# A retention layer with a phase MLP behind it: which transposes run on TensorE, which tiles go ahead, where stores are issued

## The chip, the cores and the metric

The kernel runs on one core of one Trainium2 chip. The metric is the device time of one execution in microseconds. Of the kernel before, 13 executions are known; their median is 204.08 us.

The engines of the core are called PE (matrix products, and transposes as products with an identity matrix), DVE (VectorE), ACT (ScalarE), POOL (GpSimd) and SP (SyncE, which here only issues DMAs). Each works through its own list of instructions in order. The DMA engines move data between memory and the chip, and within the chip; a DMA can also transpose a block of 16-bit numbers on the way.

## The reference, cut to what matters

```python
# q, k, v: 4 batches, 8 heads, 768 positions, 64 numbers each
for t in range(S):
    state = gamma * state + outer(k[t], v[t])        # per batch and head, 64 x 64
    y[t] = scale * q[t] @ state
x = y with the heads side by side                    # 4 x 768 x 512
theta = x @ w_theta
zr, zi = x * cos(theta), x * sin(theta)
u = x + (w_tok_r @ zr + w_tok_i @ zi)                # sums over the 768 positions of a batch
out = u + maximum(u @ w_ch, 0)
```

The second half of the work mixes all positions of a batch, so nothing of a batch's output can be computed until its retention part is complete.

## The kernel before, in words

**Tiling.** The 768 positions of a batch are six tiles of 128. Two tiles make a pair, so there are three pairs in a batch and twelve in all (n = 0 to 11, nG = 3). Output tiles are numbered m = 0 to 23, six in a batch.

**Retention, per pair.** `load` brings k, q and v of a pair (512 KB each). `prep` casts k to bf16 on ACT, and scales and casts q and v on POOL (in the first pairs half of q on DVE). q and k are then needed transposed: `flip` does it with eight TensorE transposes into PSUM and a DVE copy (kqT, L184), `flip_dma` with one DMA that transposes (L189). `ret_A` computes scores (L202), `ret_mask` masks them on DVE (L209), `ret_Y` multiplies with v (L225), `ret_I` adds the contribution of the state (L239), `ret_S` updates the state (L256) and copies it on ACT (L264). `ret_out` copies the transposed result xT out of PSUM (L273). x itself, with positions on the partitions, comes out of xT by `x_pe` (four TensorE transposes and a DVE copy, L286 and L287) or by `x_dma` (a DMA, L278).

**The MLP, per tile.** `theta` is four products (L293) and two ACT calls for cosine and sine; `zmul` multiplies them with x on DVE (L303). `moe_M` sums twelve products over the batch (L315), `moe_u` adds x on DVE (L322). u is transposed for the last product by `moe_U_dma`, a DMA (L327). `moe_O` is four products with w_ch (L333), `moe_out` the maximum and the sum on DVE, and the store, issued on SP (L340, L341).

**Weights.** `w_cast` (POOL) and `w_tok` (TensorE transposes, and copies on DVE and ACT) prepare a row block of the two token matrices.

**The order** is written out by hand and taken as it stands by each engine. First a ramp for pairs 0 to 2, line by line, with unneeded products in it (`keep_busy`). Then a loop over n = 3 to 12: slot n does the first half of pair n's retention, the second half of pair n-1's, theta and zmul of pair n-1, the MLP sums of the tiles in `tiles_of[n]`, and `moe_O` and `moe_out` of the tiles of slot n-1. Before, `tiles_of` has tiles 0 and 1 in slot 3, 2 and 3 in slot 4, 4 in slot 5, 5 in slot 6, and two in each slot after. A last loop does the six tiles of the last batch, and `moe_last` the final one.

**PSUM.** Pools are named by tag. Tag "tr" has two buffers, which `flip`, `x_pe`, `w_tok`, `moe_O` and, from pair 3 on, `theta` take in turn: a use can begin once the copy of the use two before is done. Tag "y" (the sums of `moe_M`) has one buffer.

**SP's order in a slot**, before: load k of pair n+2, the DMA transposes of u of slot n-1's tiles, that of x of pair n-1, load q, the DMA transpose of k of pair n+1, load v, that of q of pair n+1, and the stores at the end. What stands behind an instruction that waits on SP waits too.

Of the kernel before, what the change touches and what calls it, by code (L numbers as in the profile page):

```python
# [15 lines left out]
BF = mybir.dt.bfloat16  # L16
# [16 lines left out]
def kernel(  # L33
# [17 lines left out]
    nc = tc.nc  # L51
# [8 lines left out]
    gammas = [1.0 - 2.0 ** (-5.0 - h) for h in range(H)]  # L60
    nG = nT // 2

    ctx.enter_context(tc.manual_schedule())

    const = ctx.enter_context(tc.tile_pool(name="const", bufs=1))
# [30 lines left out]
    def loads(order):  # L96
        for what in order.split():
            if what == "th":
                load_w512("th", moe_w_theta)
            elif what == "ch":  # L100
                load_w512("ch", moe_w_ch)
            elif what[0] == "w":
                for r in range(2):
                    load_wtok(r, int(what[1:]))
            else:
                for name in "kqv":
                    load(int(what[1:]), name)

    loads("p0 th p1 w0 p2 w1 w2 p3 w3 p4 ch")


    warm = const.tile([P, dm], BF)
# [169 lines left out]
    def x_pe(n, a):  # L282
        b, g = divmod(n, nG)
        x_ps = psum.tile([P, NP, P], BF, name="x_ps", tag="tr", bufs=2)
        for j in range(NP):
            nc.tensor.transpose(x_ps[:, j, :], st[n, "xT"][:, a, j, :], ident)  # L286
        nc.vector.tensor_copy(xs[b][:, 2 * g + a, :], x_ps.rearrange("p j e -> p (j e)"))  # L287
# [12 lines left out]
    def zmul(n, a):  # L300
        b, g = divmod(n, nG)
        c = 2 * g + a
        nc.vector.tensor_mul(zs[b][:, c], st[n, "cs", a], _bcast_mid(xs[b][:, c, :], 2))  # L303
# [21 lines left out]
    def moe_U_dma(m):  # L325
        uT = work.tile([P, nD, P], BF, name="uT", bufs=4)
        nc.sync.dma_start_transpose(out=uT, in_=mo[m]["u"])  # L327
        mo[m]["uT"] = uT

    def moe_O(m):  # L330
        o_ps = psum.tile([P, dm], FT, name="o_ps", tag="tr", bufs=2)
        for j in range(nD):
            nc.tensor.matmul(o_ps, mo[m]["uT"][:, j, :], wch[:, j, :], start=(j == 0),  # L333
                             stop=(j == nD - 1))
        mo[m]["o"] = o_ps

    def moe_out(m):
        b, t0 = divmod(m, nT)
        ot = work.tile([P, dm], FT, name="ot", bufs=4)
        nc.vector.scalar_tensor_tensor(ot, mo[m]["o"], 0.0, mo[m]["u"], ALU.max, ALU.add)  # L340
        nc.sync.dma_start(out=out[b, t0 * P:(t0 + 1) * P, :], in_=ot)  # L341

    wrow = {}

# [18 lines left out]
    def moe_last(m):  # L363

        b, t0 = divmod(m, nT)
        hw = dm // 2
        y_ps = [psum.tile([P, hw], FT, name="y_ps", tag="y", bufs=1),
                psum.tile([P, hw], FT, name="y_ps", tag="acc", bufs=2)]
        u = work.tile([P, dm], BF, name="u", bufs=5)
        uT = work.tile([P, nD, P], BF, name="uT", bufs=4)  # L370

        def prods(e):
            for s0 in range(nT):
                for r in range(2):
                    nc.tensor.matmul(y_ps[e], wT[r][:, s0, t0 * P:(t0 + 1) * P],  # L375
                                     zs[b][:, s0, r, e * hw:(e + 1) * hw],
                                     start=(s0 == 0 and r == 0),
                                     stop=(s0 == nT - 1 and r == 1))
            nc.vector.tensor_add(u[:, e * hw:(e + 1) * hw], y_ps[e],
                                 xs[b][:, t0, e * hw:(e + 1) * hw])  # L380

        def flip_u(e):
            u_ps = psum.tile([P, 2, P], BF, name="u_ps", tag="tr", bufs=2)
            for j in range(2):
                jj = 2 * e + j
                nc.tensor.transpose(u_ps[:, j, :], u[:, jj * P:(jj + 1) * P], ident)
            nc.scalar.copy(uT[:, 2 * e:2 * e + 2, :], u_ps)

        moe_U_dma(m - 1)
        prods(0)  # L390
        moe_O(m - 2)
        moe_out(m - 2)
        prods(1)
        flip_u(0)
        moe_O(m - 1)
        moe_out(m - 1)
        flip_u(1)
        o_ps = [psum.tile([P, hw], FT, name="o_ps", tag="st", bufs=1),
                psum.tile([P, hw], FT, name="o_ps", tag="acc", bufs=2)]
        for js in ((0, 1), (2, 3)):  # L400
            for e in range(2):
                for j in js:
                    nc.tensor.matmul(o_ps[e], uT[:, j, :],
                                     wch[:, j, e * hw:(e + 1) * hw], start=(j == 0),
                                     stop=(j == nD - 1))
        for e in range(2):
            ot = work.tile([P, hw], FT, name="oh", bufs=2)
            nc.vector.scalar_tensor_tensor(ot, o_ps[e], 0.0, u[:, e * hw:(e + 1) * hw],
                                           ALU.max, ALU.add)
            (nc.sync, nc.scalar)[e].dma_start(  # L410
                out=out[b, t0 * P:(t0 + 1) * P, e * hw:(e + 1) * hw], in_=ot)
# [44 lines left out]
    w_cast(0)  # L456
    ret_A(1, 0)
    ret_mask(1, 0)
    prep(2, "k", K)
    keep_busy(2)  # L460
    ret_S(1, 0)
    zmul(0, 0)
    ret_A(1, 1)
    ret_mask(1, 1)
    ret_Y(1, 0)
    ret_I(1, 0)
    ret_S(1, 1)
    flip(2, "k")
    ret_I(1, 1)
    ret_Y(1, 1)  # L470
    ret_out(1, 0, nc.scalar.copy)
    ret_out(1, 1, nc.scalar.copy)
    prep(2, "q", DP)
    w_tok(0)
    zmul(0, 1)
    x_pe(1, 0)
    theta(1, 0)
    flip(2, "q")
    prep(2, "v", PP)
    w_cast(1)  # L480
    w_cast(2)
    x_pe(1, 1)
    theta(1, 1)
    ret_A(2, 0)
    ret_mask(2, 0)
    moe_M(0, 0, 2)
    ret_A(2, 1)
    ret_mask(2, 1)
    ret_S(2, 0)
    ret_Y(2, 0)  # L490
    ret_I(2, 0)
    ret_I(2, 1)
    prep(3, "k", K)
    ret_Y(2, 1)
    ret_out(2, 0, nc.scalar.copy)
    ret_out(2, 1, nc.scalar.copy)
    zmul(1, 0)
    w_tok(1)
    zmul(1, 1)
    prep(3, "q", DP)  # L500
    prep(3, "v", PP)
    x_pe(2, 0)
    theta(2, 0)
    moe_M(0, 2, 4)
    x_pe(2, 1)
    theta(2, 1)
    flip(3, "k")
    flip(3, "q")
    w_tok(2)
    zmul(2, 0)  # L510
    zmul(2, 1)


    tiles_of = {nG: [0, 1], nG + 1: [2, 3], nG + 2: [4], nG + 3: [5]}
    m = nT
    for n in range(nG + 4, B * nG + 1):
        tiles_of[n] = [m, m + 1]
        m += 2
    pairs = range(B * nG)
    for n in range(nG, B * nG + 1):  # L520
        mine = tiles_of[n]
        done = tiles_of.get(n - 1, [])
        late = n > nG
        if n + 2 in pairs:
            load(n + 2, "k")
        for t in done:
            moe_U_dma(t)
        if n + 1 in pairs:
            prep(n + 1, "q", PP)
            prep(n + 1, "v", PP)  # L530
        if n == nG:
            w_cast(3)
        if n in (nG + 1, nG + 2):
            w_cast(n - nG + 3)
        if n == nG + 1:
            nc.gpsimd.tensor_copy(wch, wdma["ch"])
        if late:
            ret_I(n - 1, 1)

        if n in pairs:  # L540
            ret_A(n, 0)
            ret_mask(n, 0)
        if late:
            ret_Y(n - 1, 1)
            ret_S(n - 1, 1)
            ret_out(n - 1, 0, nc.scalar.copy)
            ret_out(n - 1, 1, nc.scalar.copy)
            x_dma(n - 1)
        if n + 2 in pairs:
            load(n + 2, "q")  # L550
        if n + 1 in pairs:
            prep(n + 1, "k", K)
            flip_dma(n + 1, "k")
        if n == nG:
            moe_M(0, 4, nT)
        else:
            moe_M(mine[0], 0, nT // 2)
            theta(n - 1, 0)
            moe_M(mine[0], nT // 2, nT)
        if n == nG + 1:  # L560
            w_tok(3)
        moe_u(mine[0])
        if n + 2 in pairs:
            load(n + 2, "v")
        if n + 1 in pairs:
            flip_dma(n + 1, "q")
        if late:
            theta(n - 1, 1)
        if n == nG:
            loads("w4")  # L570
        if n == nG + 1:
            loads("w5")

        if n in pairs:
            ret_S(n, 0)
            ret_A(n, 1)
            ret_mask(n, 1)
            ret_Y(n, 0)
            ret_I(n, 0)
        if len(mine) > 1:  # L580
            moe_M(mine[1], 0, nT)
        if n in (nG + 1, nG + 2):
            w_tok(n - nG + 3)
        if late:
            zmul(n - 1, 0)
            zmul(n - 1, 1)
        if len(mine) > 1:
            moe_u(mine[1])
        for t in done:
            moe_O(t)  # L590
            moe_out(t)
# [3 lines left out]
    for m in range(last_m - nT + 1, last_m):  # L595
        if m - 1 > last_m - nT:
            moe_U_dma(m - 1)
        else:
            moe_U_dma(m - 2)
            moe_U_dma(m - 1)  # L600
        moe_M(m, 0, nT)
        moe_u(m)
        moe_O(m - 2)
        moe_out(m - 2)
    moe_last(last_m)
# [1 line left out]
_INS = ['q', 'k', 'v', 'moe_w_theta', 'moe_w_tok_r', 'moe_w_tok_i', 'moe_w_ch']  # L607
# [26 lines left out]
```

## Time and profile before

| | us |
|---|---|
| median of 13 runs | 204.08 |
| lowest and highest of them | 199.66 and 206.85 |
| the profiled execution, its own time | 206.85 |
| its span, first to last instruction | 205.1 |
| PE busy | 162.0 |
| DVE busy | 96.4 |
| ACT busy | 79.3 |
| POOL busy | 64.0 |

The profile is of one execution. Its page gives the busy time of each engine, the span in 40 slices with a digit for the busy tenths of each, the DMA traffic, the chain of work that ended last, and the costliest groups of instructions. "L202" is line 202 of the kernel. In a list of waits, "PE at_ps L202 <- DMA kqT<-kqb" means that PE, before its instruction of line 202 that writes at_ps, waited for the DMA that writes kqT; the numbers are the total in us, how often, and the longest. PEclk is the clock granted to PE, a full one being 1.00 (a 9 in the slices).

### The profile page before, as it was taken

The numbers are of one execution on the slowest core, as the hardware profiler recorded it, in microseconds if no ns is written. First come the engines' busy times: TensorE is split into PE (matmuls) and PEld (weight loads), VectorE is DVE, ScalarE is ACT, GpSimd is POOL, SyncE is SP. The second block draws the span as 40 slices with busy tenths as digits, with TensorE's granted clock in tenths as the row PEclk, the third lists the DMA queues.
The fourth block names the chain that finished last, engine by engine and source line by source line (L and its number), as shares of the span: only waits on it lengthen the run. The fifth ranks groups of instructions, "written<-read, shape, count | busy, mean of one in ns | idle before, by whom it ended". The sixth has DMA issues, their size and how long they took to land.

```text
span 205.1 us, 4473 instructions
## 1 busy us (share of the span) xinstructions
PE 162.0 (79%) x1857; PEld 86.0 (42%) x1857; DVE 96.4 (47%) x127; ACT 79.3 (39%) x136; POOL 64.0 (31%) x81
## 2 busy tenths in 40 slices
PE   7698588973199996195792896994999999899991
PEld 2354455531145543142451453453354544344470
DVE  1467577891024725228462245373065542633452
ACT  6164567640075184063650560630734624000010
POOL 5557391793716720614303305225000000000000
PEclk9999979999679999579999699997599999999999
DMA  5999999999998999989699789999434425443443
GB/s 157 332 300 333 304 338 325 272 300 176 299 193 198 287 223 210 284 187 281 178 179 192 214 178 247 232 229 246 85 72 128 80 105 100 128 106 97 135 128 105
DMA packets 82757, 41.85 MB, mean 204 GB/s; under 512 B 40112, under 2 KB 77232, under 8 KB 82736
## 3 DMA queue, kind: packets, MB, share of 16 engines
q1 hardware_dynamic: 82592, 41.43, 83.0%
q8 instruction: 14, 0.23, 0.5%
q10 hardware_dynamic: 144, 0.13, 0.2%
q14 instruction: 7, 0.06, 0.1%
HBM read 25.69 MB, written 6.29 MB: 156 GB/s over the span
## 4 chain that ended last, share of the span: by engine, by line
PE 48%; DMA 21%; SPq 11%; DVE 6%; ACT 6%; issue 5%; DVEq 0%; ACTq 0%
PE y_ps L315 20%; DMA kqT<-kqb 14%; PE th_ps L293 9%; PE o_ps L333 6%; SPq L79 5%; DMA pair<-in_k_dram 4%; SPq L189 4%; PE at_ps L202 3%; ACT stbd L264 3%; PE st_ps L256 3%; PE yT_ps L225 2%; DVE z L303 2%; DMA x_sb<-xT 1%; ACT cs L297 1%; PE y_ps L375 1%
## 5 line engine op out<-in xcount | busy, mean ns | idle before, releaser
L315 PE MATMUL y_ps<-z,wtr 128*128 128x512 bf16 x138 | 55.4, 402 | 1.2 <-DVE z L303 1.2
L315 PE MATMUL y_ps<-z,wti 128*128 128x512 bf16 x138 | 54.8, 397 | 0.0
L209 DVE TENSOR_TENSOR at<-at_ps,maskp 128x1024 bf16<-128x1024 f32 x24 | 29.3, 1222 | 31.4 <-PE at_ps L202 31.4
L173 POOL TENSOR_TENSOR kqb<-pair,qscp 128x512 bf16<-128x512 f32 x20 | 22.1, 1121 | 55.0 <-DMA pair<-in_q_dram 55.0
L322 DVE TENSOR_TENSOR u<-y_ps,x_sb 128x512 bf16<-128x512 f32 x23 | 15.9, 690 | 43.7 <-PE y_ps L315 43.7
L264 ACT CAST stbd<-st_ps 64x256 bf16<-64x256 f32 x40 | 14.6, 365 | 50.2 <-PE st_ps L256 49.7
L202 PE MATMUL at_ps<-kqT 64*64 64x128 bf16 x384 | 11.4, 234 | 27.6 <-DMA kqT<-kqb 22.9
L173 POOL TENSOR_TENSOR kqb<-pair,vscp 128x512 bf16<-128x512 f32 x24 | 25.8, 1095 | 11.8 <-DMA pair<-in_v_dram 9.5
L293 PE MATMUL th_ps<-wth,xT 128*128 128x512 bf16 x96 | 25.9, 394 | 1.0 <-ACT xT L273 0.7
L333 PE MATMUL o_ps<-wch,uT 128*128 128x512 bf16 x92 | 22.5, 379 | 2.1 <-DMA uT<-u 1.1
L273 ACT CAST xT<-yT_ps 128x512 bf16<-128x512 f32 x23 | 15.3, 733 | 19.5 <-PE yT_ps L225 19.3
L296 ACT ACTIVATE cs<-th_ps,halfpi 128x512 bf16<-128x512 f32 x24 | 16.5, 689 | 15.9 <-PE th_ps L293 15.8
L315 PEld LDWEIGHTS <-wti 128*128 128x128 bf16 x138 | 14.0, 102 | 17.2 <-issue 4.7
L315 PEld LDWEIGHTS <-wtr 128*128 128x128 bf16 x138 | 14.0, 102 | 16.8 <-issue 2.9
L303 DVE TENSOR_TENSOR z<-cs,x_sb 128x1024 bf16<-128x1024 bf16 x24 | 19.0, 826 | 4.3 <-DMA x_sb<-xT 4.3
L202 PEld LDWEIGHTS <-kqT 64*64 64x64 bf16 x384 | 8.1, 113 | 30.7 <-issue 27.7
L340 DVE SCALAR_TENSOR_TENSOR ot<-o_ps,u 128x512 f32<-128x512 f32 x23 | 15.6, 689 | 4.8 <-PE o_ps L333 3.0
L297 ACT ACTIVATE cs<-th_ps,zerob 128x512 bf16<-128x512 f32 x24 | 16.4, 683 | 0.0
L293 PEld LDWEIGHTS <-xT 128*128 128x128 bf16 x96 | 9.3, 102 | 13.0 <-issue 3.0
L167 ACT CAST kqb<-pair 128x1024 bf16<-128x1024 f32 x12 | 12.6, 1049 | 3.7 <-DMA pair<-in_k_dram 3.7
L333 PEld LDWEIGHTS <-uT 128*128 128x128 bf16 x92 | 8.7, 98 | 12.5 <-DMA uT<-u 1.6
L348 POOL CAST wrow<-wtok 128x768 bf16<-128x768 f32 x12 | 10.1, 863 | 10.4 <-PE w_ps L355 4.9
(54 smaller groups left out, 131.9 us busy)
## 6 DMA issues: line engine op xcount, KB each, us to landing
pair<-in_k_dram SPq DMA_DIRECT2D x12, 512.0 KB, 5.8
pair<-in_q_dram SPq DMA_DIRECT2D x12, 512.0 KB, 5.3
pair<-in_v_dram SPq DMA_DIRECT2D x12, 512.0 KB, 5.8
out_dram<-ot SPq DMA_DIRECT2D x23, 256.0 KB, 2.2
wtok<-in_moe_w_tok_r_dram SPq DMA_DIRECT2D x6, 384.0 KB, 6.3
wtok<-in_moe_w_tok_i_dram SPq DMA_DIRECT2D x6, 384.0 KB, 6.2
w<-in_moe_w_theta_dram SPq DMA_DIRECT2D x1, 1024.0 KB, 8.0
w<-in_moe_w_ch_dram SPq DMA_DIRECT2D x1, 1024.0 KB, 8.6
```

The lines of the kernel that those rows point to most:

```text
L173: engines[two].tensor_mul(dst[:, two], src[:, two], _bcast_last(sc[:, 2 * g + two], D))
L202: nc.tensor.matmul(at_ps[half, par, j, :], kT[rows, two, j, half], qT[rows, :, j, half], start=(j == 0), stop=(j == NP - 1), skip_group_ch ...
L209: nc.vector.tensor_mul(at.rearrange("p a j t -> p (a j) t"), at_ps.rearrange("p a j t -> p (a j) t"), _bcast_mid(maskp[:, two].rearrange(" ...
L264: nc.scalar.copy(stbd[(c + 1) % 2][sl, :, sl], st_ps[b][sl])
L293: nc.tensor.matmul(th_ps, st[n, "xT"][:, a, j, :], wth[:, j, :], start=(j == 0), stop=(j == NP - 1))
L296: nc.scalar.activation(cs[:, 0, :], th_ps, AF.Sin, bias=halfpi, scale=1.0)
L297: nc.scalar.activation(cs[:, 1, :], th_ps, AF.Sin, bias=zerob, scale=1.0)
L303: nc.vector.tensor_mul(zs[b][:, c], st[n, "cs", a], _bcast_mid(xs[b][:, c, :], 2))
L315: nc.tensor.matmul(y_ps, wT[r][:, s0, t0 * P:(t0 + 1) * P], zs[b][:, s0, r, :], start=(s0 == 0 and r == 0), stop=(s0 == nT - 1 and r == 1))
L322: nc.vector.tensor_add(u, mo[m]["y"], xs[b][:, t0, :])
L333: nc.tensor.matmul(o_ps, mo[m]["uT"][:, j, :], wch[:, j, :], start=(j == 0), stop=(j == nD - 1))
L340: nc.vector.scalar_tensor_tensor(ot, mo[m]["o"], 0.0, mo[m]["u"], ALU.max, ALU.add)
```

## The change

- Transposes of k and q are done by `flip` (TensorE) for all pairs but 10 and 11 (`KQ_DMA` = 10). Before, pairs 4 to 11 used the DMA. In the loop, k is flipped after `ret_I(n, 0)` and q after the sums of the slot's second tile.
- x is made by `x_pe` up to pair 6 (`X_DMA` = 7), before only up to pair 2.
- u is transposed on TensorE by the new `moe_U` in slots below 9 (`U_DMA` = 9), which are tiles 0 to 7; its copy is on ACT.
- Tiles 0 and 1 are summed in the ramp, ahead of pair 3. Slot 3 has tiles 2 and 3, slot 4 tile 4, slot 5 tile 5, slot 6 none.
- In the ramp, the cast of k of pair 2, the products z of the first batch, theta and the transposes of x stand at other places, `ret_out(2, 1)` copies on DVE, and two `keep_busy` products are added.
- The load of w_ch stands ahead of pair 4's, and row blocks 4 and 5 of the token matrices are loaded, cast and transposed one slot earlier (`w_ch`'s cast too).
- `store` is a function of its own. In the loop, a tile's store is issued in the middle of the slot after the one in which its output was computed. In the last tiles it follows `moe_out` as before, and the two tiles that slot 12 finishes are stored after the first sums of the last loop.

```diff
@@ -60,6 +60,8 @@
     gammas = [1.0 - 2.0 ** (-5.0 - h) for h in range(H)]
     nG = nT // 2
 
+    KQ_DMA, X_DMA, U_DMA = 3 * nG + 1, 2 * nG + 1, 2 * nG + 3
+
     ctx.enter_context(tc.manual_schedule())
 
     const = ctx.enter_context(tc.tile_pool(name="const", bufs=1))
@@ -106,7 +108,7 @@
                 for name in "kqv":
                     load(int(what[1:]), name)
 
-    loads("p0 th p1 w0 p2 w1 w2 p3 w3 p4 ch")
+    loads("p0 th p1 w0 p2 w1 w2 p3 w3 ch p4 w4")
 
 
     warm = const.tile([P, dm], BF)
@@ -327,6 +329,14 @@
         nc.sync.dma_start_transpose(out=uT, in_=mo[m]["u"])
         mo[m]["uT"] = uT
 
+    def moe_U(m):
+        u_ps = psum.tile([P, nD, P], BF, name="u_ps", tag="tr", bufs=2)
+        for j in range(nD):
+            nc.tensor.transpose(u_ps[:, j, :], mo[m]["u"][:, j * P:(j + 1) * P], ident)
+        uT = work.tile([P, nD, P], BF, name="uT", bufs=4)
+        nc.scalar.copy(uT, u_ps)
+        mo[m]["uT"] = uT
+
     def moe_O(m):
         o_ps = psum.tile([P, dm], FT, name="o_ps", tag="tr", bufs=2)
         for j in range(nD):
@@ -338,7 +348,11 @@
         b, t0 = divmod(m, nT)
         ot = work.tile([P, dm], FT, name="ot", bufs=4)
         nc.vector.scalar_tensor_tensor(ot, mo[m]["o"], 0.0, mo[m]["u"], ALU.max, ALU.add)
-        nc.sync.dma_start(out=out[b, t0 * P:(t0 + 1) * P, :], in_=ot)
+        mo[m]["ot"] = ot
+
+    def store(m):
+        b, t0 = divmod(m, nT)
+        nc.sync.dma_start(out=out[b, t0 * P:(t0 + 1) * P, :], in_=mo[m]["ot"])
 
     wrow = {}
 
@@ -390,10 +404,12 @@
         prods(0)
         moe_O(m - 2)
         moe_out(m - 2)
+        store(m - 2)
         prods(1)
         flip_u(0)
         moe_O(m - 1)
         moe_out(m - 1)
+        store(m - 1)
         flip_u(1)
         o_ps = [psum.tile([P, hw], FT, name="o_ps", tag="st", bufs=1),
                 psum.tile([P, hw], FT, name="o_ps", tag="acc", bufs=2)]
@@ -456,84 +472,89 @@
     w_cast(0)
     ret_A(1, 0)
     ret_mask(1, 0)
-    prep(2, "k", K)
     keep_busy(2)
     ret_S(1, 0)
-    zmul(0, 0)
     ret_A(1, 1)
     ret_mask(1, 1)
+    prep(2, "k", K)
     ret_Y(1, 0)
     ret_I(1, 0)
     ret_S(1, 1)
-    flip(2, "k")
     ret_I(1, 1)
+    keep_busy(2)
+    zmul(0, 0)
+    zmul(0, 1)
     ret_Y(1, 1)
     ret_out(1, 0, nc.scalar.copy)
+    w_tok(0)
     ret_out(1, 1, nc.scalar.copy)
     prep(2, "q", DP)
-    w_tok(0)
-    zmul(0, 1)
-    x_pe(1, 0)
+    flip(2, "k")
     theta(1, 0)
     flip(2, "q")
     prep(2, "v", PP)
     w_cast(1)
     w_cast(2)
-    x_pe(1, 1)
-    theta(1, 1)
+    x_pe(1, 0)
+    moe_M(0, 0, 2)
     ret_A(2, 0)
     ret_mask(2, 0)
-    moe_M(0, 0, 2)
+    theta(1, 1)
+    x_pe(1, 1)
+    ret_S(2, 0)
     ret_A(2, 1)
     ret_mask(2, 1)
-    ret_S(2, 0)
     ret_Y(2, 0)
     ret_I(2, 0)
     ret_I(2, 1)
-    prep(3, "k", K)
+    zmul(1, 0)
+    zmul(1, 1)
     ret_Y(2, 1)
     ret_out(2, 0, nc.scalar.copy)
-    ret_out(2, 1, nc.scalar.copy)
-    zmul(1, 0)
+    ret_out(2, 1, nc.vector.tensor_copy)
     w_tok(1)
-    zmul(1, 1)
+    theta(2, 0)
+    x_pe(2, 0)
+    theta(2, 1)
+    x_pe(2, 1)
+    moe_M(0, 2, 4)
+    zmul(2, 0)
+    prep(3, "k", K)
+    zmul(2, 1)
+    moe_M(0, 4, nT)
+    moe_u(0)
     prep(3, "q", DP)
     prep(3, "v", PP)
-    x_pe(2, 0)
-    theta(2, 0)
-    moe_M(0, 2, 4)
-    x_pe(2, 1)
-    theta(2, 1)
+    w_tok(2)
     flip(3, "k")
+    moe_M(1, 0, nT)
+    moe_u(1)
     flip(3, "q")
-    w_tok(2)
-    zmul(2, 0)
-    zmul(2, 1)
-
-
-    tiles_of = {nG: [0, 1], nG + 1: [2, 3], nG + 2: [4], nG + 3: [5]}
+
+
+    tiles_of = {nG - 2: [], nG - 1: [0, 1], nG: [2, 3], nG + 1: [4], nG + 2: [5], nG + 3: []}
     m = nT
     for n in range(nG + 4, B * nG + 1):
         tiles_of[n] = [m, m + 1]
         m += 2
     pairs = range(B * nG)
     for n in range(nG, B * nG + 1):
-        mine = tiles_of[n]
-        done = tiles_of.get(n - 1, [])
+        mine, done = tiles_of[n], tiles_of[n - 1]
         late = n > nG
         if n + 2 in pairs:
             load(n + 2, "k")
-        for t in done:
-            moe_U_dma(t)
+        if n >= U_DMA:
+            for t in done:
+                moe_U_dma(t)
         if n + 1 in pairs:
             prep(n + 1, "q", PP)
             prep(n + 1, "v", PP)
         if n == nG:
             w_cast(3)
-        if n in (nG + 1, nG + 2):
-            w_cast(n - nG + 3)
+            nc.gpsimd.tensor_copy(wch, wdma["ch"])
+            w_cast(4)
         if n == nG + 1:
-            nc.gpsimd.tensor_copy(wch, wdma["ch"])
+            w_cast(5)
         if late:
             ret_I(n - 1, 1)
 
@@ -545,31 +566,40 @@
             ret_S(n - 1, 1)
             ret_out(n - 1, 0, nc.scalar.copy)
             ret_out(n - 1, 1, nc.scalar.copy)
-            x_dma(n - 1)
+            if n - 1 >= X_DMA:
+                x_dma(n - 1)
         if n + 2 in pairs:
             load(n + 2, "q")
         if n + 1 in pairs:
             prep(n + 1, "k", K)
-            flip_dma(n + 1, "k")
+            if n + 1 >= KQ_DMA:
+                flip_dma(n + 1, "k")
+        if n < U_DMA:
+            for t in done:
+                moe_U(t)
+        if mine:
+            moe_M(mine[0], 0, nT // 2)
+        if late:
+            theta(n - 1, 0)
+            if n - 1 < X_DMA:
+                x_pe(n - 1, 0)
+        if mine:
+            moe_M(mine[0], nT // 2, nT)
+            moe_u(mine[0])
         if n == nG:
-            moe_M(0, 4, nT)
-        else:
-            moe_M(mine[0], 0, nT // 2)
-            theta(n - 1, 0)
-            moe_M(mine[0], nT // 2, nT)
-        if n == nG + 1:
             w_tok(3)
-        moe_u(mine[0])
         if n + 2 in pairs:
             load(n + 2, "v")
-        if n + 1 in pairs:
+        if n + 1 in pairs and n + 1 >= KQ_DMA:
             flip_dma(n + 1, "q")
         if late:
             theta(n - 1, 1)
+            if n - 1 < X_DMA:
+                x_pe(n - 1, 1)
         if n == nG:
-            loads("w4")
-        if n == nG + 1:
             loads("w5")
+        for t in tiles_of[n - 2]:
+            store(t)
 
         if n in pairs:
             ret_S(n, 0)
@@ -577,10 +607,14 @@
             ret_mask(n, 1)
             ret_Y(n, 0)
             ret_I(n, 0)
+        if n + 1 in pairs and n + 1 < KQ_DMA:
+            flip(n + 1, "k")
         if len(mine) > 1:
             moe_M(mine[1], 0, nT)
-        if n in (nG + 1, nG + 2):
-            w_tok(n - nG + 3)
+        if n + 1 in pairs and n + 1 < KQ_DMA:
+            flip(n + 1, "q")
+        if n in (nG, nG + 1):
+            w_tok(n - nG + 4)
         if late:
             zmul(n - 1, 0)
             zmul(n - 1, 1)
@@ -600,8 +634,12 @@
             moe_U_dma(m - 1)
         moe_M(m, 0, nT)
         moe_u(m)
+        if m == last_m - nT + 1:
+            store(m - 4)
+            store(m - 3)
         moe_O(m - 2)
         moe_out(m - 2)
+        store(m - 2)
     moe_last(last_m)
 # ---- launch: one core; inputs and outputs as the reference has them ----
 _INS = ['q', 'k', 'v', 'moe_w_theta', 'moe_w_tok_r', 'moe_w_tok_i', 'moe_w_ch']
```

## The prediction

> **What bounds the kernel now.** I read the page's slices first, then its DMA part, the totals of the waits, the chain that ended last, and the stages in 2 us steps.
>
> ```profile
> PE   7698588973199996195792896994999999899991
> PEclk9999979999679999579999699997599999999999
> DMA  5999999999998999989699789999434425443443
> DMA packets 82757, 41.85 MB, mean 204 GB/s; under 512 B 40112, under 2 KB 77232, under 8 KB 82736
> HBM read 25.69 MB, written 6.29 MB: 156 GB/s over the span
> ```
>
> A slice is 5.1 us. Up to slice 30 (some 145 us) the DMA engines are full while PE has holes; after it PE is full and the DMA engines are half idle. So there are two regimes, and the change must be priced in the first. 41.85 MB moved against 25.69 + 6.29 MB of HBM traffic: the other 9.6 MB are the on-chip transposes, in the small packets.
>
> ```profile
> PE at_ps L202 <- DMA kqT<-kqb: 22.9, 5, 7.7
> PE at_ps L202 <- DVE ot L340: 2.9, 1, 2.9
> 49.79 5.77 DMA kqT<-kqb
> 55.69 0.64 PE at_ps L202 x16
> 107.22 6.31 DMA kqT<-kqb
> 113.66 0.60 PE at_ps L202 x16
> 135.93 5.57 DMA kqT<-kqb
> 141.63 0.64 PE at_ps L202 x14
> ```
>
> Two totals of the waits, then steps of the chain (start, us). A pair's slot begins with its score products (L202), and five of them wait for transposed k and q: 22.9 us.
>
> ```profile
> 48.00:50.00 2.00, 0.02 (x1) 0.00 (x0) 0.53 (x1) 0.00 (x0) 0.00 (x0) 1.00 1.60 85
> 54.00:56.00 2.00, 0.31 (x13) 0.34 (x17) 0.00 (x0) 0.00 (x0) 1.88 (x2) 0.50 1.10 372
> 56.00:58.00 2.00, 2.00 (x50) 1.39 (x40) 1.22 (x1) 0.73 (x2) 0.99 (x2) 0.50 1.12 316
> 146.00:148.00 2.00, 2.00 (x6) 0.76 (x5) 0.00 (x0) 0.62 (x2) 0.00 (x0) 0.53 0.75 143
> 148.00:150.00 2.00, 2.00 (x18) 0.83 (x18) 0.69 (x1) 0.86 (x3) 0.00 (x0) 1.00 1.03 198
> 150.00:152.00 2.00, 2.00 (x58) 1.32 (x55) 1.43 (x2) 1.83 (x4) 0.00 (x0) 1.00 0.31 60
> ```
>
> Columns: stage, length, busy PE, PEld, DVE, ACT, POOL, granted clock, DMA share, GB/s. After a hole PE runs at half clock for 3 to 6 us. The last three stages carry two k/q transposes and nothing else: (0.75 + 1.03 + 0.31) x 2 = 4.2 us, so 2.1 us of all 16 engines per 256 KB.
>
> **What the Trainium skill says.** "DMA: Bandwidth & Descriptors", Specifications: below 512 B a transfer misses line rate. The trace agrees: 256 KB in 2.1 us is 125 GB/s, against slices of 338 GB/s for loads. "TensorE: Matmul & The Clock Gate", Part 4: a TensorE transpose lands in PSUM and needs a copy, and takes some 275 ns; here eight follow each other in 0.45 us (56 ns apart), so I use the trace. Same page, Part 3, What overlaps and what doesn't: matmuls are strictly in order; the trace agrees, since products ready at 48 us start at 57.2, behind the waiting scores. Same page, Why this matters for your kernels: gaps above about 3 us bring back the slow clock; here 7.7 us did, and 1.9 us at 126 did not.
>
> **What leaves the DMA engines.** Twelve k/q transposes (pairs 4 to 9) and four of x (pairs 3 to 6) at 2.1 us, eight of u (tiles 0 to 7) at half of that by bytes: 25.2 + 8.4 + 8.4 = 42 us out of 0.83 x 205.1 = 170 us. A slot's rest is three loads, 1.57 MB, and two stores, 0.52 MB: 6.4 us at 330 GB/s, against a slot of 11 to 14 us. So the DMA engines cease to bound slots 3 to 8 (slot n is the pass of the loop for pair n); slots 9 and up keep their transposes.
>
> **What arrives.** PE at full clock, from the chain: eight k or q transposes 0.45, four of x 0.22, four of u as x. Twelve, eight and eight of them: 5.4 + 1.8 + 1.8 = 9.0 us. DVE: twelve copies of 0.69 (L184) and eight of 0.41 (L287), 11.6 us. ACT: eight copies of 128x512 from PSUM; between 0.37 (128x256) and 0.80 (128x768), 0.59 taken, 4.7 us. POOL gets nothing new. All these PSUM tiles rotate through tag "tr" with two buffers, together with theta, w_tok and moe_O. That is the new wait: a use waits for the copy of the use two before, and all of PE stands behind it.
>
> **The ramp.** It contains the six last products of tile 0 and tile 1's (3.5 us that slot 3 had), and ACT's cast of k(2), which blocked the state copies by waiting 2.9 us for its load at 19.0 to 21.9 us, now stands behind them. From the second A of pair 1 (20.6) on I followed the new order with the durations above: A(2,0) at 28.3 instead of 30.6, Y(2,1) done at 32.6 instead of 34.6, tile 0 done at 39.2, tile 1 at 43.0, q(3) transposed at 43.5, copied at 44.2. Slot 3 begins at 44.4 instead of 41.15. That w_ch is loaded ahead of pair 4 delays q(4) by 1.05 MB / 0.32 = 3.3 us, from 41.4 to 44.7.
>
> **Slots.** PE's own durations: A 0.35, Y 0.22, S 0.27 to 0.30, I 0.22 (two of each a slot), theta 0.86 twice, a tile 2.59, O 0.86, w_tok 0.70.
> Slot 3: POOL starts q(4) at 44.7; q, v, cast of w row 3 need 4.4 + 1.7 us, until 50.8. PE, after scores, U(0), U(1) and tile 2, is at w_tok(3) at 47.8 and waits until 50.8 with its last half. Then 0.35 + S, A, Y, I 1.1, flip 0.45, tile 3, flip 0.45, w_tok(4) 0.70, two O: 58.5. POOL's casts of w_ch (1.9) and w row 4 (1.7) end at 54.4, before w_tok(4) at 56; the loads of w4, now in SP's first list, and of w5, now in this slot, wait on SP for POOL's casts with only the next slot's load behind. Slot of 14.1 (before 14.5).
> Slot 4, from its start: I, A, Y, S until 1.06; ACT then needs two state copies, two xT copies and the cast of k until 4.4 (in slot 7 of before the same took 99.34 to 102.34), then uT(2) until 5.0. U(2), U(3) and half a tile end at 2.8; theta takes U(2)'s buffer and waits until 5.0: 2.2 us lost. Theta and x to 6.1, half tile 7.4, theta and x 8.5, S, A, Y, I 9.7, flips to 10.6. w_tok(5) waits for DVE's flip copies behind the mask (1.22): 12.2; two O to 14.1. Before: 15.0.
> Slot 5, likewise (one tile, one U; x waits for the U copy, 1.5 us): 11.1, before 15.8. Slot 6, no tile: 11.0, before 12.0. Slot 7, two tiles and no O: 12.1, before 15.2. Slot 8, two tiles, two U, theta's 2.2 us again: 14.4, before 14.5.
> Slot 9 keeps its DMA transposes: loads 4.8, two u 2.1, x 2.1, k/q 4.2 make 13.2 us, plus landing: 13.6, before 13.5. Slot 10: 11.4 as slot 11, plus 1.0 as part of the half clock that stretched it to 14.0 before. Slot 11: 11.4.
> Sum: 44.4 + 14.1 + 14.1 + 11.1 + 11.0 + 12.1 + 14.4 + 13.6 + 12.4 + 11.4 = 158.6.
>
> **The stores** leave SP's place in front of the next slot's u transposes. SP waits 35.8 us in all for DVE's ot, with the next pair's loads and the u transposes queued behind; in slots 3 to 8 the loads have time to spare. In slot 12 it delays x_dma(11) by 1.2 us, which z, u(17) and PE follow, and at 179.84 PE waits 1.1 us for uT(16), issued behind two stores. I take 2.0 us off the 38.35 us from slot 12's start (166.75) to the end; bounds 0 and 2.5. The stores' own data (0.8 us each) lie beside PE work, and the last ones keep their place. The xT copy that moves from ACT to DVE (0.73 on either) and the two added warm-up matmuls (0.43) lie in the ramp's waits, counted within its 44.4; uncovered they cost 0.7 and 0.4.
> End: 158.6 + 36.35 = 195.0 us of span; with 206.85 - 205.1 = 1.75 around it 196.7, against 206.85. The profiled execution is 2.8 us above the median of 204.08, so the median becomes **194**.
>
> **Rivals.**
> *PE's own work alone counts* (0.17). If ACT's copies come early or PE's order covers them, the six slots 3 to 8 need PE's sums, 11.2, 10.7, 8.9, 6.3, 10.4, 12.2 = 59.7, plus 0.6 each as slot 11 shows over its sum: 63.3 instead of 76.8. Median 180.5; with half of it 187. For it: slots 11 and 12 run so. Against: they have four uses of tr, slot 4 has twelve.
> *The holes stay, with another releaser* (0.10): the first transposes wait on POOL or ACT for as long as the DMA took, or the loads (still 300 GB/s in the ramp) land late, so that slots 5 to 7 keep 14 us and lose 7.8 us of the gain: 201 to 202. For it: POOL waited 55 us for q in total. Against: q's load precedes its use by a slot.
> *Slower: the two tr buffers serialise PE* (0.07). Slot 4 has twelve uses; if each waited for the copy just before it (0.35 of PE + 0.7 + 0.1), a slot takes 13.8 us for these alone and 17 to 19 in all, six slots 25 to 30 us more: 219 to 224. It decides from 1.9 us per slot beyond my count (then nothing is gained), and from 2.5 us it is slower by 2%. Against: copies alternate between DVE and ACT, whose sums in a slot are 9.5 and 8 us.
>
> **Numbers.** Forecast 0.66, from 188 to 200. About 2% is what a measurement of this kernel tells from no change. Faster by more: 0.66 + 0.17 and a little of the second rival, 0.84; within 0.09; slower 0.07. The range leaves out the slow rival, the lowest third of the first and the top of the second: 184 to 201. It takes in the bounds of the copies (0.37 to 0.80, 1.8 us), of the stores (2.5) and of the half clock in slots 3 and 10 (0 to 2.6 each).
>
> **What will show it.** DMA share near 0.6 from 50 to 120 us; no wait of L202 for kqT but before pairs 10 and 11; slot 3 starting near 44; new waits of PE for ACT's uT copy of 1.5 to 2.2 us; slots 5 to 7 of 11 to 12 us; DVE less busy than PE in every slot. The prediction is wrong if slots 4 and 8 exceed 15 us (tr), if slot 3 starts after 48 (ramp), or if slots 3 to 8 show no tr waits (rival one).

## The result, and the profile after

The changed kernel takes 191.92 us (median; 190.72 to 196.99), the kernel before 203.78 us over 48 executions: a ratio of 0.951, with a 95% interval from 0.948 to 0.955. The forecast was 194 in 184 to 201. The profiled execution took 194.57 us, its span is 192.7. The profiled executions of both kernels are slow ones, 1.4 to 1.5% above their medians, and so are those of five of the runs below; ratios are taken from fast executions alone, medians over all.

The slices, granted clock, DMA share and packets of the changed kernel, from its page (a slice is 4.8 us):

```profile
PE   7688898688999789868898699995999999999992
PEclk9999999958999999999999999998799999999998
DMA  5999999999999903927840297499791819423443
DMA packets 61510, 36.63 MB, mean 190 GB/s; under 512 B 18864, under 2 KB 55984, under 8 KB 61488
```

From slice 14 on the DMA engines have gaps, and PE's holes of five and more us are gone. 5.2 MB less are moved: the sixteen transposes of 256 KB and eight of 128 KB. The same stretch of time in both, as stages (columns as in the prediction), first before, then after:

```profile
50.00:120.00 70.00, 49.11 (x627) 26.36 (x628) 26.86 (x33) 30.11 (x52) 26.29 (x25) 0.88 0.98 221
```

```profile
50.00:120.00 70.00, 60.53 (x934) 37.03 (x932) 42.20 (x58) 35.55 (x64) 29.82 (x29) 1.00 0.64 168
```

PE is busy for 60.5 of 70 us instead of 49.1, at a clock of 1.00 instead of 0.88, with a DMA share of 0.64 instead of 0.98. The waits of PE that answer to the 22.9 us of before:

```profile
PE th_ps L295 <- ACT uT L337: 2.8, 2, 1.7
PE at_ps L204 <- DMA kqT<-kqb: 2.0, 1, 2.0
PE th_ps L295 <- DVE ot L350: 1.6, 1, 1.6
PE x_ps L288 <- ACT uT L337: 0.9, 1, 0.9
```

One wait for a DMA transpose is left (pair 10, 2.0 us). The other three lines are the new kind: PE is held by the copy, or the output on DVE, that frees the PSUM tile it wants. Where time went, slot by slot, each from a pair's first score product to the next pair's, read in the timelines:

| slot (us) | before | forecast | after |
|---|---|---|---|
| ramp (to pair 3) | 41.1 | 44.4 | 47.6 |
| 3 | 14.5 | 14.1 | 12.0 |
| 4 | 14.9 | 14.1 | 13.8 |
| 5 | 15.9 | 11.1 | 11.0 |
| 6 | 11.9 | 11.0 | 9.3 |
| 7 | 15.2 | 12.1 | 11.5 |
| 8 | 14.5 | 14.4 | 14.3 |
| 9 | 13.5 | 13.6 | 13.1 |
| 10 | 13.9 | 12.4 | 12.6 |
| 11 and the tail | 49.6 | 47.8 | 47.5 |

### The profile page after: what moved, and what is told of

Read it like the earlier page. It is cut to its first block, busy times and chain, and to the rows that moved or that the text cites. A ratio compares the mean times of both kernels' runs of the same rounds, so it can differ in the third digit from the quotient of the medians.

```text
span 192.7 us, 4777 instructions
## 1 busy us (share of the span) xinstructions
PE 167.9 (87%) x2019; PEld 93.1 (48%) x2019; DVE 107.4 (56%) x148; ACT 82.3 (43%) x143; POOL 62.2 (32%) x81
## 4 chain that ended last, share of the span: by engine, by line
PE 66%; DVE 11%; ACT 9%; DMA 5%; issue 5%; SPq 1%; DVEq 0%; ACTq 0%
PE y_ps L317 27%; PE th_ps L295 11%; PE o_ps L343 8%; PE kq_ps L183 3%; PE at_ps L204 3%; DVE kqT L186 3%; DVE at L211 3%; DMA kqT<-kqb 3%; ACT xT L275 3%; PE st_ps L258 3%; DVE z L305 2%; ACT kqb L169 2%; PE yT_ps L227 2%; DMA pair<-in_k_dram 2%; PE yT_ps L241 2%
## 5 line engine op out<-in xcount | busy, mean ns | idle before, releaser
L317 PE MATMUL y_ps<-z,wtr 128*128 128x512 bf16 x138 | 54.0, 391 | 2.4 <-DVE z L305 1.9
L317 PE MATMUL y_ps<-z,wti 128*128 128x512 bf16 x138 | 53.9, 391 | 0.0
L175 POOL TENSOR_TENSOR kqb<-pair,qscp 128x512 bf16<-128x512 f32 x20 | 20.9, 1063 | 62.6 <-DMA pair<-in_q_dram 49.3
L324 DVE TENSOR_TENSOR u<-y_ps,x_sb 128x512 bf16<-128x512 f32 x23 | 15.9, 690 | 37.8 <-PE y_ps L317 37.8
L298 ACT ACTIVATE cs<-th_ps,halfpi 128x512 bf16<-128x512 f32 x24 | 16.6, 690 | 16.1 <-PE th_ps L295 16.1
L317 PEld LDWEIGHTS <-wti 128*128 128x128 bf16 x138 | 13.8, 100 | 17.7 <-issue 5.4
L186 DVE COPY kqT<-kq_ps 128x1024 bf16<-128x1024 bf16 x20 | 13.5, 685 | 14.4 <-PE kq_ps L183 14.4
L317 PEld LDWEIGHTS <-wtr 128*128 128x128 bf16 x138 | 13.8, 100 | 15.2 <-issue 1.7
L275 ACT CAST xT<-yT_ps 128x512 bf16<-128x512 f32 x22 | 14.9, 734 | 13.1 <-PE yT_ps L227 13.0
L305 DVE TENSOR_TENSOR z<-cs,x_sb 128x1024 bf16<-128x1024 bf16 x24 | 19.5, 850 | 0.8 <-ACT cs L299 0.5
L183 PE MATMUL kq_ps<-ident,kqb 128*128 128x128 bf16 x160 | 12.2, 224 | 3.1 <-DVE kqb L175 1.0
L204 PE MATMUL at_ps<-kqT 64*64 64x128 bf16 x384 | 10.6, 220 | 4.8 <-DVE kqT L186 2.2
L169 ACT CAST kqb<-pair 128x1024 bf16<-128x1024 f32 x12 | 12.6, 1049 | 2.7 <-DMA pair<-in_k_dram 2.7
```

The lines of the kernel that those rows point to most:

```text
L169: nc.scalar.copy(dst, src)
L175: engines[two].tensor_mul(dst[:, two], src[:, two], _bcast_last(sc[:, 2 * g + two], D))
L183: nc.tensor.transpose(ps[:, two, j, :], st[n, name][:, two, j * P:(j + 1) * P], ident)
L186: nc.vector.tensor_copy(t, ps)
L275: copy(st[n, "xT"][:, a].rearrange("e j (i w) -> e j w i", w=2), st[n, "y"][a].rearrange("e j (w i) -> e j w i", w=2))
L298: nc.scalar.activation(cs[:, 0, :], th_ps, AF.Sin, bias=halfpi, scale=1.0)
```

## The experiments

Lengths of slots below are read in the same way. L204 is the line of the score products in the changed kernel.

### Which part brings the gain

Two runs split the change. One keeps tiles, ramp, load order and stores, and gives all transposes back to the DMA:

```diff
-    KQ_DMA, X_DMA, U_DMA = 3 * nG + 1, 2 * nG + 1, 2 * nG + 3
+    KQ_DMA, X_DMA, U_DMA = nG + 1, nG, 0
```

> The changed kernel with its three thresholds set so that k, q from pair 4 on, x from pair 3 on and all u are transposed by the DMA again, as before; tiles, ramp, load order and stores stay changed. My theory (the transposes' 42 us of DMA time bound slots 3 to 8): back to 200 to 206 us. Rival (tiles 0 and 1 ahead of pair 3 and the stores' place bring the gain): 192 to 196 us.

Measured: 200.23 us (ratio 0.981, 0.950 to 1.012, so not told from the kernel before). Slots 3 to 10 last 12.2 to 14.2 us each, and the wait for k and q is back:

```profile
PE at_ps L204 <- DMA kqT<-kqb: 20.4, 7, 4.5
```

The other puts the thresholds, `flip`, `x_pe` and `moe_U` into the loop of the kernel before, with its old ramp, tiles, loads and stores:

```diff
+    KQ_DMA, X_DMA, U_DMA = 3 * nG + 1, 2 * nG + 1, 2 * nG + 3
...
-            flip_dma(n + 1, "k")
+            if n + 1 >= KQ_DMA:
+                flip_dma(n + 1, "k")
+        if n < U_DMA:
+            for t in done:
+                moe_U(t)
...
+        if n + 1 in pairs and n + 1 < KQ_DMA:
+            flip(n + 1, "k")
```

> The kernel before with the TensorE transposes alone (k, q up to pair 9, x up to pair 6, u in slots below 9), the rest as before. My theory: most of the gain, 192 to 197 us. Rival (schedule brings it): 200 us or more. A second rival, that each alone gives nothing because each uncovers the other's wait: both this and the run with all DMA transposes near 203.

Measured: 201.58 us (196.84 to 202.97 in four executions; there is no ratio). My theory fell: the transposes alone bring little. The timeline says where it goes. Pair 8 begins at 105.1 us (113.7 before, 106.8 by the forecast's slots, 105.2 in the changed kernel, whose profiled execution lost some 3 us in the ramp), so up to there the forecast gain is whole. Pair 11 begins at 151.5 instead of 145.2, and one wait on the way is

```profile
PE at_ps L204 <- DMA kqT<-kqb: 5.1, 1, 5.1
```

That pointed at the stores, which stand ahead of the next slot's DMA transposes on SP. The changed kernel with each store issued right behind its output again:

```diff
-        for t in tiles_of[n - 2]:
-            store(t)
...
             moe_O(t)
             moe_out(t)
+            store(t)
...
-        if m == last_m - nT + 1:
-            store(m - 4)
-            store(m - 3)
```

> The changed kernel with each store issued right behind its output again, as before. The prediction's step priced the stores' place at 2.0 us, all of it in the last slots: 193 to 195 us. Theory after the first runs (the kernel before with the TensorE transposes alone reached pair 8 as early as the changed kernel and lost 6 us behind it): with the stores in front, SP starts pair 10's and 11's k and q transposes late and L204 waits for them: 197 to 201 us, the loss between pairs 8 and 11. Rival (the stores' place is worth nothing): 191 to 192.5 us.

Measured: 200.13 us (ratio 0.977, 0.967 to 0.986), and most of the loss is where it was expected: pair 8 begins at 105.8, pair 11 at 149.4 (0.6 and 4.2 us later than in the changed kernel), and the rest takes 50.4 us instead of 47.5. The ramp of this execution was 3.2 us shorter; slot 3 (1.5 us longer) and slot 6 (2.3 us longer, at half clock from 86.6 us on) used that up. Slot 6 ran in part at half clock in two runs with the stores moved as well, so this part is not laid to the stores. SP's issues in slot 9 (start, us) with the stores back, where pair 9 begins at 120.4:

```profile
121.62 0.95 SPq L355 DMA_DIRECT2D out_dram<-ot  x2
122.62 0.45 SPq L81 DMA_DIRECT2D pair<-in_k_dram  x1
123.17 2.63 SPq L329 DMA_TRANSPOSE uT<-u  x2
125.89 1.26 SPq L280 DMA_TRANSPOSE x_sb<-xT  x1
127.24 0.53 SPq L81 DMA_DIRECT2D pair<-in_q_dram  x1
127.87 2.43 SPq L191 DMA_TRANSPOSE kqT<-kqb  x1
130.39 0.54 SPq L81 DMA_DIRECT2D pair<-in_v_dram  x1
131.03 2.18 SPq L191 DMA_TRANSPOSE kqT<-kqb  x1
```

and in the changed kernel, where pair 9 begins at 119.5:

```profile
111.07 1.62 SPq L81 DMA_DIRECT2D pair<-in_k_dram  x1
112.81 8.96 SPq L329 DMA_TRANSPOSE uT<-u  x2
121.87 1.26 SPq L280 DMA_TRANSPOSE x_sb<-xT  x1
123.18 0.57 SPq L81 DMA_DIRECT2D pair<-in_q_dram  x1
123.85 1.91 SPq L191 DMA_TRANSPOSE kqT<-kqb  x1
125.86 0.54 SPq L81 DMA_DIRECT2D pair<-in_v_dram  x1
126.50 3.41 SPq L191 DMA_TRANSPOSE kqT<-kqb  x1
```

Without the stores in front SP reaches the load of k 8.4 us ahead of the slot instead of 2.2 us into it, stands ready for u, and issues q's transpose 7.0 us after the slot's start instead of 10.6. L204 then waits 2.0 us instead of 5.0. So the transposes make the gain up to pair 8, and the stores' place keeps it from slot 9 on, where DMA transposes remain. The ramp and the tiles ahead seem to be worth little by themselves: with old stores, the median with them (200.13) and the one without (201.58) stand close.

### How many transposes TensorE should take

k and q by the DMA again, x and u on TensorE (`KQ_DMA = nG + 1`):

> The changed kernel with k and q of pairs 4 to 9 transposed by the DMA again (25 us of DMA time back), x and u as changed. My theory: the DMA sum of a slot is then 6.4 + 4.2 = 10.6 us against slots of 9 to 14 us, and the kqT wait at a slot's start returns in part: 196 to 202 us. Rival (x and u are what mattered): 192 to 194 us.

Measured: 189.63 us (ratio 0.940, 0.901 to 0.979); the median is 2.3 us below the changed kernel's, the ratio can't be told from its 0.951. The wait came back in small pieces only:

```profile
PE at_ps L204 <- DMA kqT<-kqb: 6.7, 5, 1.9
```

k and q on TensorE, x and u by the DMA (`X_DMA, U_DMA = nG, 0`):

> The changed kernel with x from pair 3 on and all u transposed by the DMA again (17 us of DMA time back), k and q as changed. My theory: a slot's DMA sum is 6.4 + 2.1 + 2.1 = 10.6 us, which slots of 11 to 14 us hide, while the tr waits of 1.5 to 2.2 us in slots 4, 5, 6 and 8 and 3.6 us of PE work go: 188 to 192 us, no slower than the changed kernel. Rival (all three were needed): 195 us or more.

Measured: 186.19 us (ratio 0.9225, 0.910 to 0.936), 3% faster than the changed kernel. Slots 3 to 7 take 12.7, 11.4, 9.4, 8.0 and 11.1 us. The DMA engines are nearly full again for the first 21 slices (a slice is 4.6 us):

```profile
DMA  5999999999999497999989592596864335435443
```

From 50 to 120 us their share is 0.94 here and in the run before this one, against 0.64 in the changed kernel, and PE hardly waits for them: 1.0 us for kqT here. So either half of the move ends most of the waits, although it doesn't empty the DMA engines. A full share is no bound by itself; what counts is whether a transfer lands before PE needs it. That both halves together cost more on PE and in the two tr buffers than they save on the DMA is my reading; the next runs show part of it.

Only u by the DMA (`U_DMA = 0`):

> The changed kernel with all u by the DMA, x up to pair 6 on TensorE: splits x from u. My theory (the tr waits of 1.7 and 1.0 us in slots 4 and 8 come from u's copies, those of x are small): 186.5 to 189 us. Rival (x's transposes are the costly ones): 190 to 192 us.

Measured: 189.97 us (ratio 0.929, 0.924 to 0.935). The median misses my range. By medians, giving u back to the DMA makes 2 us of the 5.7 that x and u make together; by the ratios to the kernel before it makes 4.5 of 5.9, and the interval of the run with both (0.910 to 0.936) takes in this run's ratio. The split is not settled. The timelines show 0.5 us in each of slots 4, 5 and 7 for x, as PE's 0.44 says; the other differences lie in slots 3 and 8 to 10, where x of the pair is not transposed on TensorE, and in slot 9 L204 waits 3.7 us for kqT.

The copy of u on the other engine:

```diff
-        nc.scalar.copy(uT, u_ps)
+        nc.vector.tensor_copy(uT, u_ps)
```

> The changed kernel with the PSUM copy of TensorE-transposed u on DVE, not behind the cast of k on ACT. My theory (PE stands in theta and in the x transposes for ACT's copy through the two tr buffers, 1.7 + 0.9 + 1.0 us in the profile): 187.5 to 190 us. Rival (DVE is busy there, or the next wait takes its place): 191 to 192.5 us.

Measured: 189.42 us (ratio 0.932, 0.927 to 0.936). In the changed kernel's slot 4 ACT works through this list while PE's theta stands:

```profile
60.51 0.76 ACT L266 CAST stbd<-st_ps 64x256 bf16<-64x256 f32 x2 [2.16 <-PE st_ps L258]
61.30 1.32 ACT L275 CAST xT<-yT_ps 128x512 bf16<-128x512 f32 x2
62.47 1.05 ACT L169 CAST kqb<-pair 128x1024 bf16<-128x1024 f32 x1
63.41 1.09 ACT L337 COPY uT<-u_ps 128x512 bf16<-128x512 bf16 x2
```

```profile
64.06 1.02 PE L295 MATMUL th_ps<-wth,xT 128*128 128x512 bf16 x4 [1.74 <-ACT uT L337]
```

The first fence is ACT's timeline, the second PE's; the bracket is the idle time before and its releaser. With the copy on DVE slot 4 takes 11.9 us instead of 13.8, slot 5 10.0 instead of 11.0, slot 8 13.1 instead of 14.3; slots 6 (partly at half clock) and 9 give back 1.8 and 1.1.

### The last transposes, and a hidden collision

All k and q on TensorE, x and u by the DMA (`KQ_DMA = B * nG`):

> All k and q transposes on TensorE, those of pairs 10 and 11 too; x from pair 3 on and all u by the DMA. Against the run with x and u by the DMA (186.2 us) this removes 8.4 us of DMA time in slots 9 and 10 and adds 1.8 us on PE. My theory (in that run's slot 9 L204 waited 5 us for the DMA's kqT and PE then ran at half clock): 181 to 184 us. Rival (the DMA in these slots is hidden): 186 to 188 us.

Measured: 188.77 us (ratio 0.9285, 0.924 to 0.933), a miss: no gain over 186.19 that could be told. I had read the chain's "5.01 us of DMA kqT" as a wait. The list of PE's idle times says 0.97 us; the rest ran beside PE's work. Slot 9 stayed at 11.5, and slot 10 went from 11.3 to 13.3 us, with the added flips and 1.4 us of waiting for u.

In these runs slot 8 takes 16 us. DVE, POOL and PE there, in the run with x and u by the DMA:

```profile
97.15 3.02 DVE L305 TENSOR_TENSOR z<-cs,x_sb 128x1024 bf16<-128x1024 bf16 x2
100.09 0.68 DVE L324 TENSOR_TENSOR u<-y_ps,x_sb 128x512 bf16<-128x512 f32 x1
```

```profile
96.13 2.04 POOL L175 TENSOR_TENSOR kqb<-pair,qscp 128x512 bf16<-128x512 f32 x2 [4.33 <-DMA pair<-in_q_dram]
98.13 2.94 POOL L175 TENSOR_TENSOR kqb<-pair,vscp 128x512 bf16<-128x512 f32 x2
```

```profile
100.82 0.59 PE L317 MATMUL y_ps<-z,wtr 128*128 128x512 bf16 x1 [2.64 <-DVE u L324]
```

Two z products take 3.02 us while POOL multiplies q and v, and POOL's own two take 2.94 instead of 2.04 us. The Trainium skill, "GPSIMD Engine Reference", 1. Specifications, says that POOL's SBUF interfaces are shared with VectorE and contend with its instructions that have two SBUF inputs; z has two, and the trace agrees. It shows turns, not a slowdown of both: in the changed kernel each of the six z products that began while a POOL product ran ended 0.55 us after that product's end, and one that was running when a POOL product began kept 0.69 us. u stands behind z on DVE, tag y behind u, PE behind tag y; PE then runs at a granted clock of 0.72 from 98 to 104. Issuing z ahead of q's copy (on the kernel with all k and q on TensorE):

```diff
+        if late:
+            zmul(n - 1, 0)
+            zmul(n - 1, 1)
         if n + 1 in pairs and n + 1 < KQ_DMA:
             flip(n + 1, "q")
...
-        if late:
-            zmul(n - 1, 0)
-            zmul(n - 1, 1)
```

> As the run with all k and q on TensorE, with the two products z issued ahead of the copy of q's transposes on DVE. Theory: the z products of a slot took 1.5 us instead of 0.7 each where they ran beside POOL's q products, and held u of the slot's second tile and with it tag y (2.6 us of PE in slot 8 of the run with x and u by the DMA); earlier they run while PE sums that tile: 2 to 4 us less than the run beside it. Rival (the order on DVE doesn't matter, or x's DMA isn't there yet and DVE waits): same or 1 us more.

Measured: 187.82 us (ratio 0.927, 0.921 to 0.933), not to be told from the run beside it. The mechanism is there: slot 8 takes 12.3 instead of 16.3 us, and z

```profile
99.26 1.28 DVE L305 TENSOR_TENSOR z<-cs,x_sb 128x1024 bf16<-128x1024 bf16 x2
```

But the order costs elsewhere: q's copy now waits for z and PE for that copy (1.3 us at w_tok in slot 4, 1.6 at the scores of slot 7); in slots with one tile or none there are no sums of a second tile for z to hide behind. Slot 3, 15.4 us instead of 13.5, is no part of this: no z stands there; PE waited 1.9 us for POOL's casts and then lost the clock. So z early in slots with two tiles alone, with k and q up to pair 9 on TensorE:

```diff
+        if late and len(mine) > 1:
+            zmul(n - 1, 0)
+            zmul(n - 1, 1)
...
-        if late:
+        if late and len(mine) < 2:
```

> x from pair 3 on and all u by the DMA, k and q up to pair 9 on TensorE, and in slots with two tiles the two z products ahead of the copy of q's transposes on DVE. In the run with x and u by the DMA (186.2 us) slot 8 lasted 16.1 us; with z early and all k and q on TensorE it lasted 12.3. Theory (z beside POOL's products takes 1.5 instead of 0.7 us and holds u, tag y and PE): 182 to 184 us. Rival (the order only moves the wait to an earlier slot, as in slots 3 to 5 of the other run): 186 us or more.

Measured: 182.53 us (ratio 0.896, 0.891 to 0.901), as forecast. Slot 8 lasts 12.3 us instead of 16.1. The same edit on the changed kernel itself:

> The changed kernel with the two z products ahead of the copy of q's transposes on DVE in slots with two tiles. In its profile u of the second tile is waited for 0.4 to 0.6 us in slots 8 and 9: theory 190.5 to 191.5 us, since the collision with POOL cost little here. Rival (it is as dear here as with x and u by the DMA): 187 to 189 us.

Measured: 194.71 us with a ratio of 0.947, 0.9405 to 0.953, against 0.948 to 0.955 without it: undecided, and no gain worth the name. Slot 8 keeps its 14.3 us. In the changed kernel the two z products at the start of slot 8 ran from 105.1 us and POOL's next products at 114.7: they don't meet there.

Last, the forecast's step for slot 3, that POOL's chain behind the late q(4) sets w_tok(3). In the 182.53 us kernel POOL sat idle until q(4) landed; its casts of w row 3 now fill that time:

```diff
+        if n == nG:
+            w_cast(3)
         if n + 1 in pairs:
             prep(n + 1, "q", PP)
             prep(n + 1, "v", PP)
         if n == nG:
-            w_cast(3)
```

> The fastest kernel so far (182.5 us: x and u by the DMA, z early in slots with two tiles) with POOL's casts of w row block 3 ahead of its products for q and v of pair 4 in slot 3. In that kernel's profile slot 3 lasted 15.6 us, PE waited 2.4 us at w_tok(3) for these casts and then ran at half clock for some us. The prediction's step for slot 3 says that POOL's chain behind the late q(4) sets w_tok(3): then slot 3 takes 11.5 to 12.7 us and the run 179.5 to 181.5 us. Rival (the wait is covered by the next one, pair 4's transposes): 182 to 183 us.

Measured: 180.78 us (ratio 0.892, 0.889 to 0.895), the lowest median, though the interval overlaps that of the run before (0.891 to 0.901). Slot 3 takes 11.5 us instead of 15.6; that 15.6 is the longest of the eleven profiles with the old order of POOL's casts and the new ramp (12.0 to 15.6, median 13.5). PE's timeline before this edit had

```profile
49.82 1.59 PE L369 MATMUL w_ps<-ident,wrow 128*128 128x128 bf16 x12 [2.39 <-POOL wrow L362]
```

and POOL's after it has

```profile
37.85 2.05 POOL L362 CAST wrow<-wtok 128x768 bf16<-128x768 f32 x2
44.53 2.04 POOL L175 TENSOR_TENSOR kqb<-pair,qscp 128x512 bf16<-128x512 f32 x2 [4.63 <-DMA pair<-in_q_dram]
```

The clock is 1.00 over this whole execution.

## Why the prediction was right, and what of it was not

**The sum held**, partly by luck: 195.0 us of span were forecast and 192.7 measured in an execution whose ramp was 3.2 us longer than forecast and whose slots 3 and 6 were 2.1 and 1.7 us shorter. An execution near the median (191.92 us) has a span of 190.2, so the sum is 4.8 us too long for it.

**The DMA bound in slots 3 to 8**, right: the share is 0.64, L204 waits for kqT before pair 10 alone, and with all transposes on the DMA again a slot takes 12 to 14 us. More left the DMA than had to: half was enough. Two readings were loose: the DMA engines of before are full up to slice 28, not 30 (the time given, 145 us, is right), and the slow rival's limits are 1.7 and 2.4 us per slot (from 194 to 204.08 and to 2% above it, 10.1 and 14.2 us, over six slots), not 1.9 and 2.5.

**The tr waits**, right in kind, and smaller: 1.74, 0.94 and 1.01 us at theta and x in slots 4, 5 and 8 (forecast 2.2, 1.5, 2.2). ACT's copy let PE go on 4.5 us after the slot's start in all three, 0.5 us sooner than forecast; in slot 8 PE also came 0.7 us later. Moving the copy off ACT won 2.5 us by median, 4 by the ratios. In slot 6 the wait was another one: theta waited 1.6 us for DVE's ot, behind z products that took 1.3 us each, and DVE was busier there than PE (7.6 and 6.5 us), which the forecast had excluded. Slower z beside POOL was no term of the sum.

**The ramp**, 3.2 us too short for the profiled execution: PE had half clock there,

```profile
42.00:44.00 2.00, 2.00 (x7) 0.74 (x6) 0.69 (x1) 1.03 (x1) 0.18 (x1) 0.50 1.17 296
```

and of the eleven other runs with this ramp ten have a clock of 1.00 from 36 to 46 us and pair 3 at 43.8 to 44.7 in their profile; the eleventh, with u's copy on DVE, had a clock of 0.66 as here and began it at 47.4. The clock made the difference (the last section shows what went with it); the forecast of 44.4 held where it stayed full.

**Slot 3**, 2.1 us too long in that execution: PE came late enough not to wait for POOL. In nine of the ten other runs with this order of POOL's casts PE did wait for them at w_tok(3), 0.3 to 2.4 us (forecast 3).

**The stores' place** is the step that was mis-sized. It said 2.0 us in the last slots, and that loads in slots 3 to 8 have time to spare. Both are right (47.5 instead of 49.6 us for the tail; with the stores back, slots 4, 5, 7 and 8 keep their lengths within 0.3 us). But the stores' place is worth 5 to 8 us in all (5.2 by the ratios, 7.1 by the profiled spans, 8.2 by the medians). Slot 9 had been built from DMA times (13.6) as if SP issued without delay; with the stores back, slot 9 takes 15.6 instead of 13.1 and slot 10, partly at half clock, 13.4. So the total came out right while the credit was wrong: I gave the transposes nearly all of it, and the transposes alone bring two to four us (201.58 against 203.78 over all runs of before, 205.17 in those beside it).

**The rivals.** That PE's work alone counts didn't come true here: slots 3 to 8 take 71.9 us together (forecast 76.8, rival 63.3), and the tr waits that it left out are there. Its time was reached by another kernel: with fewer transposes on TensorE, z kept apart from POOL's products, and POOL's casts early, these slots take 63.9 us and the whole 180.78. The slow rival, tr serialising PE, didn't appear: no slot exceeds 14.3 us.

## What to carry to other kernels

When a shared resource bounds a stretch, move work off it only until the next bound is met: here the half of the moved transposes that are k's and q's gave more than all. Read for each queue what stands in front of a transfer that is waited for: a store that waits for the last engine of a slot delayed every transfer behind it and cost about half of the gain. And split a change both ways, one part alone and all but one part: by the medians, two parts that gain two to five us each gained twelve together.

## What the runs showed that I had not expected

- DVE's product of two bf16 tiles (128x1024, SBUF to SBUF) takes 0.68 us alone and up to 1.57 us where POOL's own products run; POOL's pair then takes 2.94 instead of 2.04 us. The one that begins second waits for the other. DVE's instructions that read PSUM (mask 1.22, u 0.69) kept their times.
- PE's clock fell in the ramp with no gap longer than 1.1 us in front, and again after a wait of 2.0 us before pair 10, so the 3 us of the prediction are no safe bound. The fourteen traces show a pattern. Within an execution every stretch of half clock that ended lasted 3.41, 6.83 or 10.24 us, and all of them begin on one grid of 3.41 us steps, placed differently in each execution. PE's busy share, as the profile counts it, in each step of these grids from 12 us on separates the cases nearly: in all 28 steps at whose end the full clock was lost it was below 0.50, and of the 660 at whose end it was kept 646 had more (the lowest 0.40). In the ramp the step from 34.8 to 38.2 us had 0.44, and 0.45 in the other run that lost the clock; the least busy step there in the ten others had 0.48 to 0.68. The hole of 1.9 us at 126 us before the change fell across two steps (0.66 and 0.79) and kept the clock, the one of 2.0 us fell into one (0.40) and lost it.
- The time a DMA takes in the chain of waits is not what PE lost: 5.0 us of kqT stood for 0.97 us of idle PE.
